# One transformer block on one core: the fourth block's statistics on ScalarE, two projections out of the front, four beside the first block's norm

## The chip, the cores and the metric

The kernel runs on one core of one Trainium2 chip. A core has four computing engines, TensorE (PE in the profile; its weight loads are listed apart as PEld), VectorE (DVE), ScalarE (ACT) and GpSimd (POOL), and SyncE (SP), which here issues nearly all DMA transfers. Each engine runs its own instructions in order and waits for the others by semaphores. The metric is the device time of one launch in microseconds, the median of some runs.

## The reference

Everything is float32. The inputs are x (1 x 2048 x 512), a condition c (1 x 512) and the weights.

```
mod = (silu(c) @ w_mod).reshape(1, 6, 1, 512)
sa, ca, ga, sb, cb, gb = mod[:, 0], ..., mod[:, 5]
h = layernorm(x) * (1 + ca) + sa
q, k, v = heads(h @ wqkv)                 # 32 heads of 16
p = softmax(q @ k.T * 16 ** -0.5)         # full, 2048 x 2048 for each head
x = x + ga * ((p @ v) @ wo)
h = layernorm(x) * (1 + cb) + sb
x = x + gb * (gelu(h @ w1 + b1) @ w2 + b2)   # 512 -> 1792 -> 512
```

## The kernel before, in words

The 2048 rows are cut into four blocks of 512 (b = 0 to 3). Numbers that need more than the array's reduced precision are split into a high and a low part, and a product is the sum of three products of parts; a 512 x 512-row piece of a projection is then 12 matmuls of 512 columns (`terms3`, line 276 issues them). Projections are named (w, k, b): w = 0 is Q, 1 is K, 2 is V; k is one of four groups of eight heads; b is the block of rows.

**The front** is an order written out by hand, `SCRIPT`, whose tokens are run in order, each on an engine that the token may name (.v VectorE, .a ScalarE, .g GpSimd). For the tokens that matter here: `Z` loads a block of x; `S` takes the statistics of 128 rows (line 237 and 238, VectorE); `F`, `P`, `B` make the factor and the offset of the norm; `N` normalizes 128 rows; `T` transposes; `H` modulates; `I` and `L` make the high and low part of h (line 484 is `L`); `G` is one projection on the whole array; `A`, `R`, `D`, `O` split and store its result (line 508 is `D`); `K` and `Q` load K and Q back in the layout of the attention; `X` issues a pair of matmuls of scores for the row maxima (line 390), and `x` one reduction of such a tile on VectorE (line 395). Results of projections go through DRAM: `store_qk` writes the parts (lines 298 and 299), `load_rows` reads them back (line 362). The front ends when 80 maxima matmuls (`LEAD`) and their reductions are issued. The projections of the front are those that the first two units need, and some more, 13 in all.

**The attention** is one loop of 512 half-steps. A unit u is a block of 512 query rows and a group of four heads (32 units, 16 half-steps each; unit u uses query block u // 8 and head group u % 8, so k = u % 8 // 2). In a half-step TensorE issues four score matmuls for the exponentials (line 647, ScalarE's exponentials are line 654), four score matmuls for the maxima of a later unit, 80 matmuls ahead, one group of eight matmuls with V (`pv_step`, line 681), and, between them, six matmuls of a job in the background on one half of the array's rows (`bg_mm`, line 276). A job with 12 terms thus takes four half-steps. A job starts only on an even half-step. A turn (four transposes) may be added to a half-step from the list `sides`.

The counter `clock["t"]` goes up by one with each exponential, so by four in a half-step. `later(n, f)` runs f after n of them, and `soon` does the same and counts it as owed. `step_start(s)` runs at the start of a step and issues the loads in `due` whose step has come and whose projections are stored: for unit u + 2 its Q and four quarters of K, for unit u + 1 two halves of V.

**The order of the jobs** is that of the generator `work()`: `block0()` gives the projections that the front left (35), then waits until the preparation of the weights, the divisions by the softmax sums and the stores are through, and opens the pools of the feed-forward; then come, for each block, `front(b)` (four output projections, the second norm, four turns) and `feed(b)` (the feed-forward). Where the generator gives None the half-step runs without a job. For block 0, `front` runs its four turns as pieces of their own, for blocks 1 and 2 they go into `sides` beside jobs. What is not done at the end of the loop runs after it, on the whole array, ahead of the last block's output projection.

Of the kernel before, what the change touches and what calls it, by code (L numbers as in the profile page):

```python
# [16 lines left out]
P = 128  # L17
# [30 lines left out]
lw10.g be F1 L01.v H02.a L03.g W11 L00.v I02.a S22 P1 L02.v G100 S21 B1 N10.a N11.g S20 G000 N13.a R100.v  # L48
N12.a A100.v S23 D100.g F2 S31 A000.a P2 O100 T12 D000.v B2 H12.a S30 O000 T10 N22.a I12.g N23.v T13 N20.a
H10.v hw01.g N21.a H13.v T11 I10.g lw01.v I13.a T22 L10.g L12.v H11.a W20 L13.v T20 hw11.a H22.a I11.g T21 K00  # L50
# [4 lines left out]
L33.g L31.v A010.a X0*3 x R010.a G103 x D010.g x*2 O010 x*2 R103.a X0*2 x X0 A103.a G203 x D103.g x*2 O103 x*2  # L55
A203.a X0*2 x X0 G201 x*4 K03 x A201.a X0*2 x X0 K13 U201 x*2 pa1 C201 x O201 va2 pb1 x*2 vb2 X0 c1.a X0*2 x
ml1 x G111 md1 x*4 A111.a X0*2 R111.a X0 G112 x D111.g x*2 O111 x*2 A112.a X0 x X0 R112.a pa2 x D112.g x pb2 x
O112 x c2.a X1*2 x X1 mb0 x om x mb1 me0.a x U203 me1.a x*2 C203 X1*2 x X1 O203 G202 x*3 lm x*2
Y202.a X1 x*2
# [11 lines left out]
def block_kernel(ctx: ExitStack, tc: tile.TileContext, x, wqkv, wo, w1, b1, w2, b2, c, w_mod, out):  # L71
# [73 lines left out]
    pccm, pcpool = pool("pc", side="right")  # L145
    hcm, hpool = pool("hT", side="right")

# [3 lines left out]
    hT = [[rows_tile(b, "hi", "hThi"), None] for b in range(NB)]  # L151
    xin = [None] * NB
    wcm, wpool = pool("wqk", side="right")
    wslots = [wpool.tile([P, 2, KC, P], FR, name=f"wqkv{i}") for i in range(4)]
# [21 lines left out]
    def load_x(b, q=sy):  # L176

        xin[b] = rows_tile(b, "lo", "xin", (P, 4, D), F32)
        for t in range(0, 4, 1 if b == 0 else 4):
            r0, n = b * TB + t * P, 1 if b == 0 else 4  # L180
            q.dma_start(xin[b][:, t : t + n], x[r0 : r0 + n * P, :].rearrange("(t p) d -> p t d", p=P))
# [111 lines left out]
    stored = set()  # L293

    def store_qk(w, k, b, parts):
        stored.add((w, k, b))
        planes = qk_d[w][k].rearrange("i d o t -> (d o) i t")[:, :, b * TB : (b + 1) * TB]
        sy.dma_start(planes[:, 1 - w : 3 - w], parts.bitcast(F32))
        sy.dma_start(planes[:, 2 * w], parts[:, 0].bitcast(F32))
# [30 lines left out]
    def turn_v(bk, apart=False):  # L330
# [12 lines left out]
        def store():  # L343
            stored.add((2, k, b))
            (ac if apart else sy).dma_start(v_d[2 * k : 2 * k + 2, :, 4 * b : 4 * b + 4, :].rearrange("g p k e -> p g k e"), vst)
# [106 lines left out]

    def power(b):
        gp.tensor_tensor(rs1[b], rs1[b], mhalf, op=ALU.pow)
# [26 lines left out]
    def low_x(b, f, e):  # L481
        if hT[b][1] is None:
            hT[b][1] = rows_tile(b, "lo", "hTlo")
        e.tensor_tensor(hT[b][1][:, f], keep.pop(("H", b, f)), hT[b][0][:, f].bitcast(F32), op=ALU.subtract)
# [73 lines left out]
    def high_later(w, k, b, e):  # L558
# [8 lines left out]
        "S": lambda b, t: ln_stat(mv1[b], t, xin[b][:, t]), "F": add_eps, "P": power, "B": offset, "N": norm1,  # L567
# [26 lines left out]
    vg, pt = {}, {}  # L594

    def load_v(u, h):
        assert all((2, u % NG // 2, b) in stored for b in (2 * h, 2 * h + 1))
        if h == 0:
            vg[u] = vgpool.tile([P, NKC, VG], F32, tag="vg", name="vg")
        sl = slice(8 * h, 8 * h + 8)  # L600
        sy.dma_start(vg[u][:, sl], v_d[u % NG][:, sl])

    load_v(0, 0)
# [70 lines left out]
    def pv_step():  # L674
        s = cur["pv"]
        cur["pv"] += 1
        u, kc = divmod(s, NKC)
        if kc == 0:
            cur["ps"] = take("pv")
# [137 lines left out]
    def front(b, x2):  # L817
# [9 lines left out]

        def norm(t):
            xn[t] = tmp("xn")
            (gp if b or t < 3 else ve).tensor_scalar(  # L830
                xn[t], x2[t], mv[:, t, 0:1], rs[t], op0=ALU.subtract, op1=ALU.mult)
            later(40, lambda: gp.tensor_tensor(x2[t], x2[t], b2_b, op=ALU.add))
            if b and len(xn) == 4:
                later(9, lambda: sides.extend([lambda fc=fc: trans(fc, "mx") for fc in range(KC)]))

        def stat(t):
            if b == 0 and t == 3:
                ln_stat(mv, t, x2[t])
                later(1, lambda: factor(t))
                return  # L840
# [10 lines left out]
            later(4, lambda: part(1))  # L851
            later(8, whole)

        def factor(t):
# [3 lines left out]
            later(3 if t < 3 else 2, lambda: norm(t))  # L858

        for t in range(4):  # L860

            def evac(ps, t=t):
# [3 lines left out]
                def add():  # L866
                    gp.tensor_tensor(x2[t], y, x2[t], op=ALU.add)
                    later(8 if b or t < 3 else 3, lambda: stat(t))
# [5 lines left out]
        t0 = clock["t"]  # L874

        def trans(fc, bk="bg"):
# [11 lines left out]
        if b:  # L888
            yield from until(lambda: len(turned) == KC and clock["t"] >= turned[KC - 1] + 8)
            return  # L890
        yield from until(lambda: len(xn) == 4 and clock["t"] >= t0 + 9)
        for fc in range(KC):
            yield lambda fc=fc: trans(fc)
        yield from wait(4)

    def feed(b, x2):
# [4 lines left out]
        def piece(i):  # L901
            return f.tile([P, 2, TB], FR, tag="g", name="g", bufs=8)
# [66 lines left out]
    def block0():  # L969

        plan = [(1, 1, [3]), (2, 1, [0, 1, 2, 3])]
        plan += [(w, k, range(1 if w == 0 else NB)) for k in (2, 3) for w in (0, 1, 2)]
        plan += [(0, k, range(1, NB)) for k in range(KC)]

        def fetch(n):
            if n < len(plan):
                w, k, _ = plan[n]
                load_w(w, k)
                soon(12, lambda: split_w(w, k, wslots[n % 4]))
# [3 lines left out]
        for n, (w, k, bs) in enumerate(plan):  # L983
            if not pcs and not any(0 in p[2] for p in plan[n:]):
                open_pc()
            yield from until(lambda: (w, k) in wt_of)
            fetch(n + 2)
            for b in bs:
                yield proj_v(k, b) if w == 2 else proj_qk(w, k, b)
            wt_of.pop((w, k))  # L990
        yield from until(lambda: not preps and not owed[0] and not vrows and not busy[0])
        open_ffn()
# [5 lines left out]
    def work():  # L998

        yield from block0()  # L1000
        fronts = [front(b, pools["x2"][b % 2]) for b in range(NB - 1)]
        for b in range(NB - 1):
            for j in fronts[b]:
                if j != "ln":
                    yield j
            for j in feed(b, pools["x2"][b % 2]):
# [39 lines left out]
    def half_step(hs):  # L1046
# [4 lines left out]
        h = hs % 2  # L1051
        if h or len(wt) < len(used) + KC:
            wload()
# [93 lines left out]
    due = [(1, [(2, 0, 2)], lambda: load_v(0, 1))]  # L1147

    def step_start(s):
        u, kc = divmod(s, NKC)  # L1150
        for d in [d for d in due if d[0] <= s and all(k in stored for k in d[1])]:
            due.remove(d)
            d[2]()
        if kc == 0 and u + 2 < NU:
            g = (u + 2) % NG // 2
            due.append((16 * u + 4, [(0, g, (u + 2) // NG)], lambda: load_q(u + 2)))
            for b, n in enumerate((5, 8, 14, 16)):
                t0 = b % 2 * TB
                due.append((16 * u + n, [(1, g, b)], lambda b=b, t0=t0: load_k(u + 2, b // 2, t0, t0 + TB)))
        if kc == 0 and u + 1 < NU:  # L1160
            for h in range(2):
                need = [(2, (u + 1) % NG // 2, b) for b in (2 * h, 2 * h + 1)]
                due.append((16 * u + 2 + h, need, lambda h=h: load_v(u + 1, h)))
# [116 lines left out]
    close(tcm, pools["cm"], pccm, kqcm)  # L1280
# [24 lines left out]
```

## Time and profile before

| | |
|---|---|
| median of 3 runs | 1687.93 us (1685.45 to 1688.35) |
| the profiled execution, its time | 1688.23 us |
| its span in the profile | 1686.4 us |
| mean granted TensorE clock | 0.996 |
| busy: TensorE, VectorE, ScalarE, GpSimd | 1666.6, 1402.0, 1242.7, 691.2 us |
| front, loop, tail (by the trace) | 0 to 100.35, to 1562.67, to 1686.40 us |

Busy time is the time in which an engine had an instruction in work. The chain of waits follows, from the last instruction back, what released each step; its shares tell where the span went. A line number belongs to the helper that issues the instruction, so the tile's names tell which step it is. Matmuls are pipelined, so TensorE's busy time doesn't say that it is at its peak.

### The profile page before, as it was taken

To read this page: it belongs to the slowest core of one execution; us is meant where nothing else is said; L and a number is where in the kernel's file an instruction comes from. 1 tells how busy PE (TensorE), PEld (TensorE's weight loads), DVE (VectorE), ACT (ScalarE), POOL (GpSimd) and SP (SyncE) were. 2 spreads that over 40 slices of the span, in tenths; PEclk is the share of its full clock that TensorE was granted. 3 is DMA by queue.
4 is the path that set the end of the run, shared out by engine and by line. 5 is a ranking of instruction groups with operands and counts; after the bars stand their busy time and mean duration, and the time that the engine had idled before them with its cause. 6 is when DMAs were issued, how large, how long until landed. Compare 5 with 4: busy or idle time off the path is not lost.

```text
span 1686.4 us, 32218 instructions
## 1 busy us (share of the span) xinstructions
PE 1666.6 (99%) x12103; PEld 915.8 (54%) x12103; DVE 1402.0 (83%) x2686; ACT 1242.7 (74%) x2386; POOL 691.2 (41%) x697
## 2 busy tenths in 40 slices
PE   7999999999999999999999999999999999999999
PEld 6655555555554455555545555555555555553777
DVE  7998888889889989888999888888999888890332
ACT  4367888878777788778877888778877788779131
POOL 7333534425121456415633456306633466226110
PEclk8999999999999999999999999999999999999999
DMA  8766766756457443425453464344363453243544
GB/s 291 220 195 186 236 194 200 227 182 206 146 159 215 121 106 102 106 67 150 123 162 88 114 165 121 84 133 134 105 181 86 116 144 101 75 119 97 209 153 157
DMA packets 137127, 251.88 MB, mean 149 GB/s; under 512 B 25854, under 2 KB 45324, under 8 KB 136972
## 3 DMA queue, kind: packets, MB, share of 16 engines
q1 hardware_dynamic: 135984, 248.53, 50.9%
q8 instruction: 96, 1.57, 0.4%
q10 hardware_dynamic: 988, 1.29, 0.3%
q14 instruction: 59, 0.48, 0.1%
HBM read 188.49 MB, written 61.28 MB: 148 GB/s over the span
## 4 chain that ended last, share of the span: by engine, by line
PE 95%; DMA 2%; DVE 1%; ACT 1%; issue 0%; POOL 0%; SPq 0%; DVEq 0%; POOLq 0%; ACTq 0%
PE bg L276 40%; PE pv L681 30%; PE e L647 16%; PE mx L390 5%; PE pr L276 2%; ACT p L654 1%; DVE mxp L395 1%; DMA wraw<-in_A_wqkv_dram 1%; PE o L276 1%; PE mx L335 0%; DMA wo<-wos 0%; DMA kh<-qk 0%; PE mx L879 0%; DMA xin<-in_A_x_dram 0%; POOL wqkv L208 0%
## 5 line engine op out<-in xcount | busy, mean ns | idle before, releaser
L395 DVE TENSOR_REDUCE mxp<-mx 128x1 f32<-128x512 f32 x2034 | 1286.4, 683 | 145.7 <-PE mx L390 131.4
L654 ACT ACTIVATE p<-e 128x512 f32<-128x512 f32 x2048 | 1072.8, 608 | 272.2 <-PE mx L390 251.4
L390 PE MATMUL mx<-kh,qst 48*128 48x512 f32 x2034 | 836.6, 423 | 0.7 <-DVE mxp L395 0.5
L647 PE MATMUL e<-qst,kh 50*128 50x512 f32 x2048 | 779.2, 424 | 3.2 <-ACT p L654 3.2
L647 PEld LDWEIGHTS e<-qst,kh 50*128 50x128 f32 x2048 | 341.8, 185 | 431.5 <-ACT p L654 310.2
L681 PE MATMUL pv<-p,vg 128*32 128x512 f32 x4096 | 547.2, 605 | 0.3 <-ACT osb L668 0.3
L390 PEld LDWEIGHTS mx<-kh,qst 48*128 48x128 f32 x2034 | 368.2, 185 | 14.2 <-DVE mxp L395 8.3
L276 PE MATMUL bg<-w,g 64*128 64x512 f32 (+1 forms) x1056 | 264.3, 389 | 0.8 <-issue 0.8
L276 PEld LDWEIGHTS bg<-w,g 64*128 64x128 f32 (+1 forms) x1056 | 196.0, 186 | 30.0 <-issue 1.2
L276 PE MATMUL bg<-pchi,w 64*128 64x512 f32 (+1 forms) x656 | 177.6, 391 | 0.0
L681 PEld LDWEIGHTS pv<-p,vg 128*32 128x32 f32 x4096 | 81.1, 108 | 173.0 <-issue 160.3
L276 PE MATMUL bg<-hThi,wqkv 64*128 64x512 f32 x560 | 153.1, 392 | 0.0
L276 PEld LDWEIGHTS bg<-pchi,w 64*128 64x128 f32 (+1 forms) x656 | 120.9, 185 | 23.9 <-DVE tick L1091 4.2
L276 PEld LDWEIGHTS bg<-hThi,wqkv 64*128 64x128 f32 x560 | 103.7, 185 | 12.7
L923 POOL TENSOR_SCALAR s<-s 128x512 f32<-128x512 f32 x40 | 59.9, 1497 | 90.3 <-ACT s L921 89.6
L942 POOL TENSOR_TENSOR x<-y,x 128x512 f32<-128x512 f32 x28 | 36.0, 1286 | 144.6 <-ACT y L941 128.7
L276 PE MATMUL bg<-pclo,w 64*128 64x512 f32 (+1 forms) x328 | 88.9, 389 | 0.0
L276 PE MATMUL bg<-hTlo,wqkv 64*128 64x512 f32 x280 | 76.5, 392 | 0.0
L276 PEld LDWEIGHTS bg<-pclo,w 64*128 64x128 f32 (+1 forms) x328 | 60.0, 184 | 13.5 <-DVE tick L1091 4.2
L916 POOL TENSOR_TENSOR s<-h 128x512 f32<-128x512 f32 x40 | 41.7, 1042 | 61.7 <-ACT h L915 61.7
L276 PE MATMUL bg<-wo,pchi 64*128 64x512 f32 x192 | 59.5, 389 | 0.4 <-DMA wo<-wos 0.4
L276 PEld LDWEIGHTS bg<-hTlo,wqkv 64*128 64x128 f32 x280 | 51.6, 184 | 7.5
(163 smaller groups left out, 1322.9 us busy)
## 6 DMA issues: line engine op xcount, KB each, us to landing
kh<-qk SPq DMA_DIRECT2D x256, 192.0 KB
w<-w1s SPq DMA_DIRECT2D x56, 512.0 KB
w<-w2s SPq DMA_DIRECT2D x54, 512.0 KB
vg<-v SPq DMA_DIRECT2D x64, 332.0 KB
qk<-parts SPq DMA_DIRECT2D x32, 512.0 KB
qst<-qk SPq DMA_DIRECT2D x64, 192.0 KB
qk<-parts SPq DMA_DIRECT2D x32, 256.0 KB
ou<-osb SPq DMA_DIRECT2D x32, 256.0 KB
```

The lines of the kernel that those rows point to most:

```text
L276: return te.matmul(ps, term[0][r], term[1][r], start=i == 0, stop=i == n - 1)
L390: te.matmul(ps, qst[u][r0 : r0 + KR, p, qc * P : (qc + 1) * P], kh(u, kr // 2)[r0 : r0 + KR, p, (kr % 2) * TB : (kr % 2 + 1) * TB], start= ...
L395: ins = ve.tensor_reduce(mxp[u][:, hc, kr : kr + 1], ps, axis=AX.X, op=ALU.max, negate=True)
L647: ins = te.matmul(ps, kh(u, kc // 8)[r0 : r0 + KX, p, (kc % 8) * P : (kc % 8 + 1) * P], qst[u][r0 : r0 + KX, p], start=True, stop=True)
L654: op = ac.activation(t, ps, AF.Exp, scale=SCALE)
L681: te.matmul(cur["ps"][32 * j : 32 * (j + 1)], vg[u][:, kc, j * VW : j * VW + 32], pt.pop(4 * s + j), start=kc == 0, stop=kc == NKC - 1)
L916: gp.tensor_tensor(s, h, h, op=ALU.mult)
L923: gp.tensor_scalar(s, s, 1.0, None, op0=ALU.add)
L942: later(4, lambda: gp.tensor_tensor(x2[t], y, x2[t], op=ALU.add))
```

## The change

In the front the sums and the sums of squares of the fourth block's rows are taken on ScalarE, by activations with a summed output (tokens `E`, `V`), and GpSimd and VectorE make mean and variance of them (`J`, `f`). The projections G111 and G112 (K of head group 1 for blocks 1 and 2) leave the front and become jobs of the loop. The reductions are spaced anew, and the first maxima matmuls come ahead of G110. The fourth block's h and the four weight slots lie in the eight tiles that the feed-forward uses later (`piece_tile`), so they may live past the opening of its pools. In the loop the order of the projections is written out, and the four Q projections of block 3 are set aside (`deferred`); they run wherever block 0's path would give None, and the pools are opened from the half-step itself (`try_open`). Block 0's norm of its last 128 rows takes its statistics in halves, normalizes on GpSimd, and its turns go into `sides`. Loads of K and Q now wait until six exponentials after the store's issue, those of V until four, and V is loaded in quarters for the units that need a fresh projection.

```diff
-N12.a A100.v S23 D100.g F2 S31 A000.a P2 O100 T12 D000.v B2 H12.a S30 O000 T10 N22.a I12.g N23.v T13 N20.a
+N12.a A100.v V30 V31 V32 S23 D100.g F2 A000.a P2 O100 T12 D000.v B2 H12.a O000 T10 N22.a I12.g N23.v T13 N20.a
...
-H20.a I22.g L11.v I20.a lw11.g T23 H21.a K10 S32 G101 I21.g Q0 H23.a L22.v I23.a Q1 L20.v L23.g G110 L21.v
-A101.a S33 hw20.a lw20.g F3 D101.v P3 R110.a X0*2 O101 A110.a x X0 B3 G200 x D110.g N32.a x N30.a x N31.g O110
+H20.a I22.g L11.v I20.a lw11.g T23 H21.a Q0 f3 G101 I21.g H23.a L22.v I23.a K10 L20.v L23.g X0*2 Q1 G110 x L21.v x
+A101.a hw20.a lw20.g x R101.a D101.g P3 R110.a X0 x O101 A110.a x X0*2 B3 G200 x D110.g N32.a x N30.a x N31.g O110
...
-ml1 x G111 md1 x*4 A111.a X0*2 R111.a X0 G112 x D111.g x*2 O111 x*2 A112.a X0 x X0 R112.a pa2 x D112.g x pb2 x
...
+    def row_sum(b, t):
+        o = kqpool.tile([P, TB], F32, tag="osb", name="junk", bufs=1)
+        ac.activation(o, xin[b][:, t], AF.Identity, accum_out=sums[:, 0, t : t + 1])
...
+    def row_var(b, t):
+        o = kqpool.tile([P, TB], F32, tag="osb", name="junk", bufs=1)
+        ac.activation(o, xin[b][:, t], AF.Square, bias=sums[:, 1, t : t + 1], accum_out=sums[:, 2, t : t + 1])
...
         def norm(t):
             xn[t] = tmp("xn")
-            (gp if b or t < 3 else ve).tensor_scalar(
-                xn[t], x2[t], mv[:, t, 0:1], rs[t], op0=ALU.subtract, op1=ALU.mult)
+            gp.tensor_scalar(xn[t], x2[t], mv[:, t, 0:1], rs[t], op0=ALU.subtract, op1=ALU.mult)
...
-            if b and len(xn) == 4:
-                later(9, lambda: sides.extend([lambda fc=fc: trans(fc, "mx") for fc in range(KC)]))
+            if len(xn) == 4:
+                later(9 if b else 6, lambda: sides.extend([lambda fc=fc: trans(fc, "mx") for fc in range(KC)]))
...
-            later(4, lambda: part(1))
-            later(8, whole)
+            later(2 if short(t) else 4, lambda: part(1))
+            later(4 if short(t) else 8, whole)
...
-        plan = [(1, 1, [3]), (2, 1, [0, 1, 2, 3])]
-        plan += [(w, k, range(1 if w == 0 else NB)) for k in (2, 3) for w in (0, 1, 2)]
-        plan += [(0, k, range(1, NB)) for k in range(KC)]
+        plan = [(1, 1), (2, 1), (0, 2), (1, 2), (2, 2), (0, 3), (1, 3), (2, 3)] + [(0, k) for k in range(KC)]
+        order = [(0, 1), (0, 2), (0, 3), (1, 0), (1, 1), (1, 2), (1, 3), (2, 0), (3, 0), (3, 1), (3, 2), (3, 3),
+                 (4, 0), (4, 1), (4, 2), (5, 0), (6, 0), (4, 3), (6, 1), (6, 2), (6, 3),
+                 (7, 0), (7, 1), (7, 2), (8, 1), (7, 3), (8, 2), (9, 1), (9, 2), (10, 1), (10, 2), (11, 1), (11, 2)]
...
+    def filled(js):
+        for j in js:
+            yield proj_late() if j is None and deferred else j
+
+    def try_open():
+        if over0[0] and "f" not in pools and not preps and not owed[0] and not vrows and not busy[0]:
+            open_ffn()
...
-        for d in [d for d in due if d[0] <= s and all(k in stored for k in d[1])]:
+        for d in [d for d in due if d[0] <= s and all(clock["t"] >= stored.get(k, 1 << 30) + d[2] for k in d[1])]:
             due.remove(d)
-            d[2]()
+            d[3]()
...
-                due.append((16 * u + n, [(1, g, b)], lambda b=b, t0=t0: load_k(u + 2, b // 2, t0, t0 + TB)))
+                due.append((16 * u + n, [(1, g, b)], 6, lambda b=b, t0=t0: load_k(u + 2, b // 2, t0, t0 + TB)))
```

In `order` each pair is a place in `plan` and a block of rows; counted from 0, the nth pair is the loop's nth job.

More of the change, by code (lines that the diff above doesn't have):

```diff
@@ L887, in front @@
         yield "ln"
[L888 to L894, printed above, removed]
+        yield from until(lambda: len(turned) == KC and clock["t"] >= turned[KC - 1] + (8 if b else 5))
     def feed(b, x2):
@@ L991, in block0 @@
-        yield from until(lambda: not preps and not owed[0] and not vrows and not busy[0])
-        open_ffn()
+            yield from until(lambda: plan[n] in wt_of)
+            fetch()
+            w, k = plan[n]
+            yield proj_v(k, b) if w == 2 else proj_qk(w, k, b)
+            left.pop(0)
+            if n not in left and n < len(plan) - KC:
+                wt_of.pop((w, k))
+        deferred.extend((k, gslots[(len(plan) - KC + k) % 4]) for k in range(KC))
+        over0[0] = True
@@ L1051, in half_step @@
         h = hs % 2
+        try_open()
         if h or len(wt) < len(used) + KC:
```

138 lines of the change are left out of this document (87 added, 51 removed).

## The prediction

> **What bounds the kernel now.** I read the page first, then the share of each engine by stretch, then the chain of waits, then single instructions on VectorE's, ScalarE's and SyncE's timelines.
>
> ```profile
> span 1686.4 us, 32218 instructions
> PE 1666.6 (99%) x12103; PEld 915.8 (54%) x12103; DVE 1402.0 (83%) x2686; ACT 1242.7 (74%) x2386; POOL 691.2 (41%) x697
> PE 95%; DMA 2%; DVE 1%; ACT 1%; issue 0%; POOL 0%; SPq 0%; DVEq 0%; POOLq 0%; ACTq 0%
> ```
>
> TensorE is busy 99% of the span and carries 95% of the chain, so the kernel falls into stages that all end with TensorE, and a moved piece is worth what its old place gives back less what its new place takes.
>
> ```profile
> 0.00:47.42 47.42, 38.50 (x211) 30.06 (x213) 38.51 (x68) 20.44 (x31) 36.59 (x45) 0.89 0.87 277
> 47.42:100.35 52.93, 51.94 (x259) 32.17 (x255) 50.07 (x86) 18.70 (x35) 15.36 (x17) 1.00 0.71 221
> 100.35:1562.67 1462.32, 1457.37 (x11116) 757.67 (x11116) 1273.48 (x2469) 1176.56 (x2282) 627.71 (x626) 1.00 0.50 140
> ```
>
> The columns are stretch, length, then busy time (and instructions) of PE, PEld, DVE, ACT, POOL. In the second row, the half of the front that holds the row maxima, TensorE works 51.94 of 52.93 us, but VectorE works 50.07. Two limits lie 1.9 us apart there: taking work from TensorE alone soon uncovers VectorE. In the attention (third row) VectorE has room: 1273 of 1462 us.
>
> **The change part by part.**
>
> *Two projections leave the front (G111, G112).* A projection there is 12 matmuls, alone on the array:
>
> ```profile
> 47.84 3.00 PE pr L276 x12
> 40.53 0.68 DVE L237 BATCH_NORM_STATS2 bst<-xin 128x6 f32<-128x512 f32 x1
> 41.34 3.92 DVE L484 TENSOR_TENSOR hTlo<-h,hThi 128x512 fp32r<-128x512 f32 x3
> 45.18 0.68 DVE L237 BATCH_NORM_STATS2 bst<-xin 128x6 f32<-128x512 f32 x1
> 46.12 0.58 DVE L451 TENSOR_SCALAR rs<-mv 128x4 f32<-128x4 f32 x1
> 46.62 0.68 DVE L508 TENSOR_TENSOR parts<-pr,parts 128x512 fp32r<-128x512 f32 x1
> 47.42 3.68 DVE L395 TENSOR_REDUCE mxp<-mx 128x1 f32<-128x512 f32 x6
> ```
>
> On TensorE 2 x 3.00 = 6.0 us go. The 80 row-maximum matmuls and their 80 reductions stay in the front, respaced. VectorE loses four statistics (0.68 each and an aggregate), one rest (0.68) and one subtraction that goes to GpSimd; one subtraction that stood before the first reduction (a third of the 3.92 us, 1.31) now comes after it, and the one that leaves the second stretch is taken at 0.91 by me (an estimate between the 0.68 and the 1.31). So from the first reduction to the loop VectorE has 50.07 - 0.91 + 1.31 = 50.5 us of work. The first maximum matmuls now stand behind one projection (G101) and not two, so the first reduction comes about 2.8 us earlier (3.00, less an estimated 0.2 for Q's rows, whose load SyncE now puts out just ahead of their use). If VectorE idles in between as much as before (52.93 - 50.07 = 2.9), the front ends 2.8 - 0.4 = 2.4 us earlier; if it idles not at all, 5.3. That is all of the 6.0 that can be had.
>
> *ScalarE takes the fourth block's statistics.* Four sums, four squares. The nearest rows are its normalizations, also with pointers for scale and offset:
>
> ```profile
> 31.23 0.60 ACT L192 ACTIVATE parts<-pr 128x512 fp32r<-128x512 f32 x1 [1.80 <-PE pr L276]
> 32.72 2.23 ACT L464 ACTIVATE xin<-xin,nb,rs 128x512 f32<-128x512 f32 x3 [0.23 <-POOL nb L459]
> ```
>
> That is 0.74 us each; the sum that is written out as well is in no row, so I bound one at 0.60 to 1.00 and take 0.85. The four sums go into an earlier gap. Three squares stand ahead of the evacuation at 31.23, in a gap of 1.80: 3 x 0.85 - 1.80 = 0.75 us late (0 to 1.2). Behind it wait the rest on VectorE, the bank, and the transposition that needs the bank; the fourth square then stands ahead of the third block's modulations. VectorE's missing statistics give part of this back. I charge 0.9 us to all that follows (0 to 1.5). The two small GpSimd operations and the split load of x on SyncE lie under the sums. The front is worth 2.4 - 0.9 = -1.5 us (from -5.3 to +0.2).
>
> The Trainium skill (ScalarE: Activation LUTs, What ACT_TABLE_LOAD costs) prices an ACTIVATE with one pointer at 280 ns + 0.833 ns an element, less 93 ns back to back: 0.61 us here, an estimate that leaves out the written sum. By it the three squares about fit the 1.80 gap and the front would be worth some 2.3 us; the rows at 0.74 speak against so little.
>
> *The stretch around the first block's norm.* In the loop a projection takes four half-steps (24 half-row matmuls, six each). Before: 35 projections fill half-steps 0 to 139, six half-steps idle (the last store, then the loads of wo), 146 to 161 hold four output projections, and eight idle ones hold the norm, with four turns.
>
> ```profile
> 484.88:507.65 22.77, 22.77 (x182) 11.94 (x178) 20.54 (x40) 17.51 (x35) 7.00 (x8) 1.00 0.43 134
> 507.65:523.47 15.82, 14.37 (x102) 5.00 (x98) 15.09 (x27) 13.13 (x26) 2.12 (x4) 1.00 0.57 171
> 523.47:569.98 46.51, 46.11 (x358) 24.06 (x354) 43.43 (x89) 35.37 (x69) 9.56 (x9) 1.00 0.59 163
> 569.98:594.88 24.90, 23.40 (x150) 9.04 (x146) 21.84 (x39) 19.55 (x37) 13.93 (x14) 0.93 0.63 155
> 509.39:512.00 2.61, 2.40 (x20) 0.83 (x24) 2.53 (x5) 2.07 (x5) 0.46 (x3) 1.00 0.08 13
> 583.54:586.44 2.90, 2.90 (x25) 1.25 (x22) 2.33 (x4) 2.37 (x5) 1.53 (x3) 1.00 0.45 138
> 528.22:531.72 3.50, 3.10 (x27) 1.33 (x30) 2.90 (x6) 2.44 (x6) 0.00 (x0) 1.00 1.04 406
> 584.50 0.59 PE bg L879 x4
> 1562.67 16.57 PE bg L276 x72
> 1580.06 3.01 PE bg L276 x12
> ```
>
> A filled half-step costs 22.77 / 8 = 2.85 us, an idle one 2.61, an idle one with a turn 2.90: filling an idle slot costs 0.24 us. That is why moving work here is cheap. After: 33 projections (0 to 131); three of the four deferred ones until the store, the softmax divisions, four ticks and the loads of wo are through (132 to 143); outputs 144 to 159; the last deferred one 160 to 163. By the new delays the first turn comes 20 exponentials, five half-steps, after the last output; turns at 164 to 167, two idle, and the feed-forward starts at 170, as before. So the jobs behind it stay, and the number that overrun the loop (84 / 12 = 7 of 12 matmuls, the last two rows). Sum over 132 to 169: 12 x 2.85 + (46.51 - 0.65 for the load of wo that ended late, the 3.50 us half-step) + 4 x 2.85 + 4 x 3.05 + 2 x 2.61 = 108.9, against 22.77 + 15.82 + 46.51 + 24.90 = 110.0: -1.1 us. A turn goes at 3.05, between 2.90 and 2.61 + 0.59 of transposes; -1.8 to +1.5 if new norm waits show. The halved statistics and GpSimd's normalization of the fourth row go under deferred work; without that cover they cost what the 24.90 row has over 8 x 2.61, up to 4 us.
>
> *What the two late projections do to SyncE.* All K and V of the loop come up to eight half-steps later, and loads now also wait six exponentials after the store. The maxima run 80 ahead, 4 a half-step; unit 6 needs K of its second 512 rows at 6 x 64 + 16 = 400 = 80 + 4 x 80, half-step 80. That K projection now is job 18, half-steps 72 to 75. Before, job 18 was the K of the fourth rows, so its rows show when such a load can go out:
>
> ```profile
> 100.35:333.82 233.47, 84.17 (x632) 12.45 (x632) 1.00 0.68 206
> 321.45 0.60 ACT L310 ACTIVATE pf<-bg 128x512 f32<-128x512 f32 x1
> 326.84 0.57 SPq L422 DMA_DIRECT2D qst<-m  x2
> 327.92 0.43 SPq L298 DMA_DIRECT2D qk<-parts  x1
> 328.40 0.45 SPq L299 DMA_DIRECT2D qk<-parts  x1
> 332.65 2.13 SPq L362 DMA_DIRECT2D kh<-qk  x2
> SPq L362 <- DMA qk<-parts: 1.4, 2, 0.9
> 53.09 1.74 SPq L362 DMA_DIRECT2D kh<-qk  x4
> 57.66 0.29 PEld L390 LDWEIGHTS mx<-kh,qst 48*128 48x128 f32 x3 [0.17 <-DMA kh<-qk]
> ```
>
> 632 / 8 = 79 PV groups have run by 333.82: there half-step 80 starts. The store goes out at 327.92, behind the maxima's rows; the load waited for it until 332.65. Before, its data had until half-step 88. Now they are wanted at once: with the 57.66 - 53.09 = 4.57 us from issue to use seen in the front they land at 337.2, 3.3 us late. TensorE stands, with everything behind it. Bounds: 0, if the load goes out earlier, to three times 3.3 (the third and fourth rows' K, half-steps 84 and 88, have the same distance, but the first stand gives them its 3.3 us and no maxima's rows are in front of them: I charge them 0.2). V of units 4 and 6, loaded in quarters, has over two half-steps: nothing; the two more issues a unit (0.45 us each, as at 328.40) fit SyncE's gaps.
>
> The Trainium skill (DMA: Bandwidth & Descriptors, Anatomy of one DMA) gives 2.0 us + bytes / 436e3 per DMA; two of 192 KB, one issue apart, would land about 2.9 us after the first issue, an estimate for another issuing path. By it the stand is 1.8 us and the sum 1687.6; the trace's 4.57 decides.
>
> *Sum.* -1.5 - 1.1 + 3.3 + 0.2 = +0.9 us on the profiled execution's 1688.23, that is 1689.1; it lies 0.3 above the median 1687.93, so 1688.8. No change that a measurement can tell: about 0.2%, 3.4 us, is what it resolves here.
>
> **The rivals.** *The K load is in time* (SyncE runs ahead of TensorE, and the store finds no maxima's rows in front): then -1.5 - 1.1 = -2.6; with half of VectorE's 2.9 us of idling gone too, -4.1, 1683.8, faster. For it: in the waits of 320 to 345 us, the quoted row, SyncE stood 0.9 us at the longest for such a store. Against: 332.65 is a measured time for this very slot. Chance 0.26.
>
> *The K loads are late again and again*, slower: the second and third stand full as well, 3 x 3.3 - 2.6 = +7.3, 1695.2; it decides from the second on (+4.0, 1691.9). For it: evacuation at 321.45 to issue at 332.65 is 11.2 us, and with 4.57 more 15.8; the four half-steps between are 11.4. Against: in the other two nothing holds the store back but GpSimd. Chance 0.26. The Trainium skill (same page and section) says that a DMA's completion is told only when its last byte is confirmed in the target memory, long above all with HBM; the 4.73 us from store to dependent load agree.
>
> *ScalarE's statistics eat the front*: one at 1.0 us with VectorE idle as before, front +0.2; then 1690.5, still no change. Chance 0.08.
>
> **Chances.** The forecast (one stand of about 3 us, front and middle some 2.6) 0.40, with 0.08 for the last rival: 0.48 within 0.2%. Faster 0.26, slower 0.26. Range 1683.0 to 1693.5: the low end takes the K load in time with part of the front's bound, the high end two full stands and a little more.
>
> **What the profile would show.** Right: VectorE without a gap before the loop, the loop's first exponentials 1 to 2 us earlier; a wait of TensorE's maxima on the K load near half-step 80; half-steps 132 to 143 all full; no wait on wo; the feed-forward at half-step 170. Wrong: no such wait; a front shorter by over 3 us; an overrun of the loop by six jobs or eight instead of seven.

## The result, and the profile after

The change made the kernel slower. The median went from 1688.14 us (four runs, 1685.45 to 1688.77) to 1710.76 us (four runs, 1703.86 to 1712.29); the ratio is 1.0129, with a 95% interval of 1.0100 to 1.0159. The prediction was 1688.8 us, with a range from 1683.0 to 1693.5. The profiled execution took 1712.29 us, at a mean granted clock of 0.989 (0.996 before).

From the page of the changed kernel: the span, the busy time by engine, the chain by engine, and the group of the maxima's matmuls (at the end of that row: the idle time of TensorE just ahead of them, and what ended most of it).

```profile
span 1710.5 us, 32286 instructions
PE 1676.3 (98%) x12127; PEld 922.1 (54%) x12127; DVE 1396.8 (82%) x2682; ACT 1248.5 (73%) x2401; POOL 697.4 (41%) x704
PE 91%; DMA 4%; ACT 2%; DVE 1%; POOL 1%; issue 1%; SPq 0%; DVEq 0%; POOLq 0%; ACTq 0%
L414 PE MATMUL mx<-kh,qst 48*128 48x512 f32 x2038 | 842.7, 424 | 17.1 <-DMA kh<-qk 14.3
```

TensorE is busy 10 us longer than before, although the two projections only changed their place (in the loop each is 24 matmuls on half of the array's rows), and the chain now runs through transfers for 4% of the span (2% before). The maxima (line 414, line 390 before) stood 14.3 us for K. By stretch (columns as in the prediction; until the first reduction, then until the loop, then the loop):

```profile
0.00:44.25 44.25, 35.26 (x199) 27.53 (x199) 32.78 (x58) 24.96 (x46) 35.52 (x45) 0.92 0.88 291
44.25:112.15 67.90, 55.03 (x250) 33.50 (x247) 50.27 (x86) 18.61 (x34) 20.09 (x20) 0.90 0.52 157
112.15:1587.79 1475.64, 1467.45 (x11164) 765.18 (x11164) 1273.73 (x2475) 1177.90 (x2283) 630.26 (x629) 0.99 0.49 140
```

The span grew by 24.1 us. The first reduction comes 3.2 us earlier, but the stretch from there to the loop takes 67.90 us and not 52.93, with the same 50 us of VectorE's work in it: VectorE idles 17.6 us. The loop takes 13.3 us more, the rest, the tail, 1.0 less.

The front on TensorE, instructions in order of time (start, length; in brackets the idle time ahead and what ended it):

```profile
57.36 1.05 PE L414 MATMUL mx<-kh,qst 48*128 48x512 f32 x6 [2.11 <-DMA kh<-qk]
...
69.52 0.60 PE L414 MATMUL mx<-kh,qst 48*128 48x512 f32 x2 [2.02 <-DMA kh<-qk]
70.05 3.18 PE L300 MATMUL pr<-h,wqkv 128*128 128x512 f32 x8
...
86.79 1.31 PE L414 MATMUL mx<-kh,qst 48*128 48x512 f32 x4 [5.09 <-DMA kh<-qk]
...
91.93 3.36 PE L300 MATMUL pr<-hThi,wqkv 128*128 128x512 f32 x8
...
104.33 2.11 PE L300 MATMUL pr<-hThi,wqkv 128*128 128x512 f32 x8
...
112.15 0.79 PE L414 MATMUL mx<-kh,qst 48*128 48x512 f32 x1 [2.27 <-DVE mxp L419]
...
119.75 1.93 PE L724 MATMUL pv<-p,vg 128*32 128x512 f32 x8
```

Three of the waits are for K of unit 0's second, third and fourth 512 rows; the fourth is for a reduction on VectorE. And eight matmuls of a projection, 2.11 us at 104.33, take 3.18 and 3.36 us behind two of the waits. The granted clock (the third number from the end of a row) shows why; behind the fourth wait the loop's first steps are slow too:

```profile
70.00:80.00 10.00, 10.00 (x45) 6.81 (x48) 5.99 (x10) 1.68 (x3) 1.29 (x1) 0.83 0.40 150
70.78:74.20 3.42, 3.42 (x10) 2.66 (x9) 0.54 (x1) 0.00 (x0) 0.00 (x0) 0.50 0.57 214
80.00:90.00 10.00, 4.91 (x27) 2.91 (x20) 4.61 (x9) 0.60 (x1) 0.00 (x0) 0.72 0.65 178
111.74:121.98 10.24, 9.83 (x41) 5.58 (x43) 6.62 (x12) 4.73 (x9) 0.19 (x1) 0.50 0.22 70
```

The clock is at one half from 70.78 to 74.20, from 84.44 to 94.68 and from 111.74 to 121.98 us, that is for 3.4 us or three times that.

The chain of waits through the third stand, step by step:

```profile
75.92 1.30 POOL parts L549
...
77.24 0.36 SPq L322
...
77.65 5.04 DMA qk<-parts
...
83.11 3.54 DMA kh<-qk
...
86.79 1.31 PE mx L414 x4
```

K goes from a projection to its maxima through memory: split, store (5.04 us until it is confirmed), load (3.54 us), 12.1 us from the projection's end (74.67) to the use. In the kernel before the way is as long: K of the second rows is used some 13.7 us after the end of its projection in both kernels (at 57.66 before, a row of the prediction, at 57.36 now). Before, other work filled it.

The loop: half-steps 80, 84 and 88, in which the maxima on unit 6's second, third and fourth rows begin, and 81, behind the first of them (a filled half-step is 2.85 us, with a turn 3.50):

```profile
349.05:355.48 6.43, 3.89 (x25) 2.03 (x23) 3.10 (x6) 3.25 (x7) 4.75 (x5) 0.89 0.46 134
355.48:359.28 3.80, 3.80 (x23) 1.60 (x23) 2.06 (x5) 2.08 (x5) 0.22 (x1) 0.73 0.09 36
364.97:369.35 4.38, 3.29 (x24) 1.73 (x22) 2.50 (x6) 2.90 (x7) 1.88 (x2) 1.00 1.04 263
377.99:384.83 6.84, 5.38 (x27) 3.15 (x27) 3.94 (x7) 3.62 (x7) 2.22 (x3) 0.75 0.84 248
```

Over 2.85 us (3.50 for the last, which holds a turn) that is 3.6 + 0.9 + 1.5 + 3.3 = 9.3 us; with 0.5 at half-step 60 and 0.2 at 92 the loop lost 10.0 us on K. TensorE's waits for K are 2.54, 1.09 and 1.46 us of this; the clock is at one half again from 354.09 to 357.50 and from 381.40 to 384.81 us. Four more it lost at its start, at the low clock: 7.6 us from 112.15 to the first PV group (4.5 before) and 1.0 in the half-step after it.

### The profile page after: what moved, and what is told of

Its sections match the earlier page's. It is cut to its first block, busy times and chain, and to the rows that moved or that the text cites. A ratio compares the mean times of both kernels' runs of the same rounds, so it can differ in the third digit from the quotient of the medians.

```text
span 1710.5 us, 32286 instructions
## 1 busy us (share of the span) xinstructions
PE 1676.3 (98%) x12127; PEld 922.1 (54%) x12127; DVE 1396.8 (82%) x2682; ACT 1248.5 (73%) x2401; POOL 697.4 (41%) x704
## 4 chain that ended last, share of the span: by engine, by line
PE 91%; DMA 4%; ACT 2%; DVE 1%; POOL 1%; issue 1%; SPq 0%; DVEq 0%; POOLq 0%; ACTq 0%
PE bg L300 39%; PE pv L724 29%; PE e L689 15%; PE mx L414 5%; DMA qk<-parts 1%; DMA kh<-qk 1%; ACT p L696 1%; DVE mxp L419 1%; PE pr L300 1%; DMA wraw<-in_A_wqkv_dram 1%; PE o L300 1%; PE mx L359 1%; PE mx L919 0%; DMA wf<-in_B_w_dram 0%; ACT xin L505 0%
## 5 line engine op out<-in xcount | busy, mean ns | idle before, releaser
L414 PE MATMUL mx<-kh,qst 48*128 48x512 f32 x2038 | 842.7, 424 | 17.1 <-DMA kh<-qk 14.3
L300 PEld LDWEIGHTS bg<-pchi,w 64*128 64x128 f32 (+1 forms) x656 | 120.9, 185 | 24.1 <-DVE tick L1157 4.2
L300 PE MATMUL bg<-hThi,wqkv 64*128 64x512 f32 x432 | 120.5, 400 | 0.0
L300 PEld LDWEIGHTS bg<-hThi,wqkv 64*128 64x128 f32 x432 | 82.1, 191 | 10.2
L435 POOL CAST m<-mt 128x32 fp32r<-128x32 f32 x32 | 6.7, 209 | 145.5 <-DVE mt L433 145.5
L300 PE MATMUL bg<-hTlo,wqkv 64*128 64x512 f32 x216 | 58.0, 388 | 0.0
```

What stands on the lines that cost most here:

```text
L300: return te.matmul(ps, term[0][r], term[1][r], start=i == 0, stop=i == n - 1)
L414: te.matmul(ps, qst[u][r0 : r0 + KR, p, qc * P : (qc + 1) * P], kh(u, kr // 2)[r0 : r0 + KR, p, (kr % 2) * TB : (kr % 2 + 1) * TB], start= ...
L435: gp.tensor_copy(m2[:, 0], mt)
```

## The experiments

All ratios are to the kernel before, run on the same chip in the same series, with 95% intervals.

**1. The front whole again, two jobs less in the loop.** The front's order of before stands in the changed kernel; the late Q projections, the pools' opening, the delays and V in quarters stay.

```diff
-        order = [(0, 1), (0, 2), (0, 3), (1, 0), (1, 1), (1, 2), (1, 3), (2, 0), (3, 0), (3, 1), (3, 2), (3, 3),
+        order = [(0, 3), (1, 0), (1, 1), (1, 2), (1, 3), (2, 0), (3, 0), (3, 1), (3, 2), (3, 3),
```

> Edit: the changed kernel with the front's order of before (13 projections, all statistics on VectorE) and without the two extra jobs in the loop; the four late projections of the first block and the new loads stay. Theory (all of the loss comes from the two projections that left the front): no maximum waits over 0.6 us for K in the front or in half-steps 60 to 92; the front as before, the stretch of half-steps 132 to 169 as in the changed kernel, 0.7 us shorter than before; about 1687.4 us. Rival (the late four, the quartered V loads or the longer delays cost time by themselves): stands remain in the loop, 1692 or more.

Measured: 1688.64 us, ratio 1.0008 (0.9999 to 1.0018): no difference. From its page: all maxima together stood 1.1 us, most of it for reductions, none to speak of for K.

```profile
L414 PE MATMUL mx<-kh,qst 48*128 48x512 f32 x2030 | 834.9, 422 | 1.1 <-DVE mxp L419 1.0
```

So the loss hangs on the two projections that left the front, with the order that the front was given for it. The late four, the delays and V in quarters cost nothing that can be measured, and bring nothing either.

**2. The front whole, all 33 jobs in the loop.** Only the front's order is that of before.

> Edit: the changed kernel with the front's order of before, all 13 projections in it, while the loop still holds all 33 of its jobs, so that two projections are computed twice (the loop's copies overwrite equal rows). It has the loop of the changed kernel behind the front of before. Theory (the loop's stands come from the two jobs more, whatever the front does): first PV group at 104 to 105 us, waits of the maxima on K at half-steps 60, 80, 84 and 88 as in the changed kernel, 8 to 10 us together; about 1696 us. Rival (the front's lateness pushes SyncE and GpSimd back, and the loop's stands come from that): stands under 3 us together, 1690 or less.

Measured: 1695.72 us, ratio 1.0051 (1.0036 to 1.0065). First PV group at 103.86 us, and the stands are there, with the low clock behind the first:

```profile
331.86:338.00 6.14, 3.29 (x25) 1.72 (x23) 2.49 (x6) 2.89 (x7) 4.27 (x5) 1.00 0.49 125
338.00:342.42 4.42, 4.42 (x23) 2.03 (x23) 2.90 (x6) 2.77 (x7) 0.68 (x1) 0.61 0.26 103
```

From half-step 60 to 92 the loop fell back 7.4 us, so most of the loop's loss does not come from the front. With experiment 1 this splits the result: 0.43% (some 7 us) for the two jobs more in the loop, 0.78% (1.0129 less 1.0051, some 13 us) for the front; the interval of the changed kernel's ratio alone leaves 5 us to either side of the second.

**3. Another order of the maxima in the front.** Three pairs of unit 1 (K there already) take the place of the first pairs on unit 0's second rows.

```diff
-N33.a x*2 A200.a X0*2 x X0 G102 K01 x*2 K11 x*3 A102.a X0*2 x X1 T30 D102.v x O102 T32 H30.a x I30.g T33 H32.a
+N33.a x*2 A200.a X0*2 x X0 G102 K01 x*2 K11 x*3 A102.a X1*2 x X1 T30 D102.v x O102 T32 H30.a x I30.g T33 H32.a
...
-X0 pa2 x X0 pb2 x*3 c2.a mb0 om me0.a X1*2 mb1 x X1 me1.a x*2 G202 lm x*3 X1*2 Y202.a x*2 X1*2 x*6
+X0 pa2 x X0 pb2 x*3 c2.a mb0 me0.a X0*2 mb1 x X1 me1.a x*3 om G202 lm x*2 X1*2 Y202.a x*2 X1*2 x*6
```

> Edit: the changed kernel with another order of the same 40 pairs of maxima in the front: three of unit 1, whose K is there, stand where the first maxima on unit 0's second rows stood; unit 0's last two come later for it. Theory (TensorE runs into loads of its own fresh K, and runs at half clock after each stand): the stands of 2.1, 2.0 and 5.1 us go or shrink to under 1.5 us together, no record at a clock of 0.5 between 65 and 105 us, first PV group 9 to 13 us earlier than 119.75; some 1699 us, since the loop's stands stay. Rival (VectorE is the bound and the stands only show it): the waits turn into waits on reductions, first PV group less than 4 us earlier, 1708 or more.

Measured: 1699.33 us, ratio 1.0071 (1.0056 to 1.0086), first PV group at 109.44. Two of the three stands are gone, the third is 2.21 us:

```profile
81.43 1.31 PE L414 MATMUL mx<-kh,qst 48*128 48x512 f32 x4 [2.21 <-DMA kh<-qk]
```

With the same work on every engine, an order in which TensorE asks for fresh K later gives back some 10 us: 1.0129 less 1.0071 is 0.58%, and the first PV group comes 10.3 us earlier (8.2 earlier than in the profile of experiment 6, whose front is the changed kernel's). (The clock behind the third stand still fell, to 0.66 in the mean of 80 to 90 us, which was expected not to happen.) VectorE was not the bound.

**4 and 5. The waits filled.** Small matmuls of no use ahead of the three waiting maxima (`WARM`: 12, 12, 30, then 9, 8, 21).

```diff
+        for n in range(WARM.get((u, i), 0) * a):
+            te.matmul(ps[:, :P], ident, ident, start=True, stop=True)
```

> Edit: the changed kernel with 12, 12 and 30 small matmuls (128x128 on the identity, about 0.15 us each) ahead of the three maxima of the front that wait for K, into the bank that these overwrite. They do no work; the data come no earlier. Theory (the clock falls because TensorE idles): no record at 0.5 between 65 and 105 us, the projections at 70.05 and 91.93 take 3.0 us instead of 4.6 and 4.2, and the first PV group starts 3 to 6 us earlier; 1705 to 1708 us. Rival (the clock falls for another reason): the records stay, and the time is that of the changed kernel or more.

> Edit: the changed kernel with 9, 8 and 21 small matmuls of no use ahead of the three maxima of the front that wait for K (12, 12 and 30 ran over the arrival of the last K by 3 us: each leaves two records of 0.115 us). Theory (TensorE's idling makes the clock fall; with the stands filled to 0.3 us each it does not): granted clock 1.00 from 50 to 105 us, the maxima on the last K at 86 to 87 us as in the changed kernel, the first PV group 3 to 4 us earlier than 119.75; some 1707 us. Rival (the fall of the clock costs nothing, since VectorE's reductions bound that stretch): first PV group at 119 us or later, 1710 or more.

Measured: 1708.49 us (1.0126, 1.0111 to 1.0141) and 1706.74 us (1.0111, 1.0098 to 1.0125). In the first the filling ended at 89.68 us, some 3 us behind the start of those maxima in the changed kernel (86.79), so its gain was given away and the expected time missed. The second, by stretch:

```profile
70.00:80.00 10.00, 9.80 (x54) 6.93 (x57) 7.20 (x12) 1.69 (x3) 2.82 (x3) 1.00 0.39 139
80.00:90.00 10.00, 10.00 (x80) 7.29 (x73) 6.27 (x13) 1.26 (x3) 0.00 (x0) 1.00 0.80 248
```

The clock stays at 1.00 where the changed kernel had 0.83 and 0.72, the maxima on the last K start at 86.93 us, no earlier than before, and the first PV group starts at 116.34 us, 3.4 earlier. How much of this is the clock is less sure than it looks: in the profile of experiment 6 the same front brought the first PV group at 117.61. That kernel's four times, taken in the same series, lie 3.4 us higher in the median (1710.15) and don't overlap with these, but its loop lost 1.7 us more. So of the front's 15 us some 1.3 to 3.4 were the low clock behind the K waits, and that clock follows TensorE's idling. The Trainium skill (TensorE: Matmul & The Clock Gate, Part 1: The HAM clock gate, and Why this matters for your kernels) says that the clock halves after an idle window of about 3.4 us and advises against gaps over some 3 us; the trace agrees with the half rate and with 3.4 us as its step, but here stands of 1.46 to 2.54 us were enough in several places (not in all: the first, 2.11 us, left the clock at 1.00).

**6. No delay ahead of the K loads.**

```diff
-                due.append((16 * u + n, [(1, g, b)], 6, lambda b=b, t0=t0: load_k(u + 2, b // 2, t0, t0 + TB)))
+                due.append((16 * u + n, [(1, g, b)], 0, lambda b=b, t0=t0: load_k(u + 2, b // 2, t0, t0 + TB)))
```

> Edit: the changed kernel in which the loop's K loads no longer wait six exponentials after the issue of their store (they still wait for its landing). Theory (job, evacuation, split, store and landing are too long a chain for four or five half-steps, and the delay lies beside the store's landing of 3 to 5 us): the stands at half-steps 60 to 92 change by less than 2 us in sum; 1709 to 1711 us. Rival (the added delay makes the stands): each shrinks by the 4 us of six exponentials, to under 3 us in sum; 1703 or less.

Measured: 1710.15 us, ratio 1.0133 (1.0120 to 1.0146). Half-steps 60 to 92 lost 11.7 us, no less than with the delay. The chain itself is too long:

```profile
337.77 0.67 ACT pf L334
...
339.18 1.29 POOL parts L336
...
344.31 0.42 SPq L322
...
344.79 4.09 DMA qk<-parts
...
349.32 3.62 DMA kh<-qk
...
353.08 0.47 PE mx L414
```

These are lines of the changed kernel's chain. From evacuation to use 15.3 us pass, of which four half-steps (11.4 us) are there; 3.8 us of it SyncE's queue holds the finished store back, behind the rows of the maxima (`m`, `qst`) and a weight.

**7. One projection back in the front.**

```diff
-c1.a X0*2 x X0 ml1 x*2 md1 U201 x*2 C201 x O201
+G112 c1.a A112.a R112.a X0*2 x D112.g X0 ml1 x*2 md1 O112 U201 x*2 C201 x O201
...
-        order = [(0, 1), (0, 2), (0, 3), (1, 0), (1, 1), (1, 2), (1, 3), (2, 0), (3, 0), (3, 1), (3, 2), (3, 3),
+        order = [(0, 1), (0, 3), (1, 0), (1, 1), (1, 2), (1, 3), (2, 0), (3, 0), (3, 1), (3, 2), (3, 3),
```

> Edit: the changed kernel with one of the two projections (second head group, third rows) back in the front, ahead of the maxima that wait 5.1 us, and out of the loop's list. Theory (with one more job in the loop unit 6's K is in time, with two it is not): the stands at half-steps 80, 84 and 88 go (under 0.5 us each), the loop gives back 8 to 10 us; the front's own stands stay, though the new projection fills 3 of the 5.1 us; about 1700 us. Rival (unit 6's K is late because of SyncE's order or of the six exponentials of delay, not for the one job more): stands of over 1 us remain at half-steps 80 and 84, 1705 or more.

Measured: 1705.45 us, ratio 1.0103 (1.0086 to 1.0120). The loop's stands on K are gone, as the theory had it (the front keeps two, of 2.03 and 1.97 us); but the time is the rival's, for a new stand came (half-steps 80 and 144; then, in order of time, GpSimd's division and the first scores behind it):

```profile
346.31:349.16 2.85, 2.85 (x25) 1.51 (x24) 2.48 (x5) 2.55 (x6) 2.77 (x3) 1.00 0.58 164
531.63:540.61 8.98, 4.45 (x26) 2.92 (x24) 3.28 (x6) 3.31 (x7) 2.21 (x4) 0.67 0.72 211
```

```profile
526.31 1.28 POOL L790 TENSOR_TENSOR ob<-ob,rb 128x512 f32<-128x512 f32 x1 [14.64 <-DMA rb<-rden]
...
537.22 0.76 PE L689 MATMUL e<-qst,kh 50*128 50x512 f32 x1 [4.53 <-DMA qst<-m]
```

GpSimd stood 14.64 us for the sums of a softmax division (2.04 us in the changed kernel), the cast of unit 9's maxima stood behind it, and the first scores of unit 9 waited for them.

**8. to 11. A version without these stands.** Experiment 8 joins the order of 3 with the projection of 7, and issues the divisions later; 9 also moves the fourth rows' chain forward in the front; 10 holds the loads of the feed-forward's weights back until the divisions are issued; 11 respaces the front's end.

```diff
-            later(9 if over[0] else 7, div)
+            later(9 if over[0] else 12, div)
```

> Edit: the changed kernel with the other order of maxima, one projection back in the front ahead of the maxima on the last K (and out of the loop), and GpSimd's softmax divisions issued five exponentials later, so that GpSimd does not stand in front of the cast of unit 9's maxima. Theory (both causes are mended: no loads of fresh K in the front, unit 6's K in time, and the stand at half-step 144 was GpSimd's queue): no wait over 1 us for K anywhere, none at half-step 144; first PV group at 107 to 109 us, and from there on within 1.5 us of before; 1689 to 1692 us. Rival (the loop holds a further cost of the late projections): a stand over 2 us elsewhere, 1694 or more.

Measured: 1703.68 us, ratio 1.0102 (1.0085 to 1.0119): a miss. K waits are under 0.4 us, but the stand at half-step 144 stayed (7.94 us), so a later issue of the division was no cure, and the front lost time to a load of `w_mod` that the earlier order now met (1.93 us, with a clock of 0.58 from 90 to 100 us): its first PV group came at 115.36 us, not at 107 to 109.

The front of experiment 9, shortened to the tokens that move:

```diff
-A101.a hw20.a lw20.g x R101.a D101.g P3 R110.a X0 x O101 A110.a x X0*2 B3 G200 x D110.g N32.a x N30.a x N31.g O110
+A101.a hw20.a lw20.g x R101.a D101.g R110.a X0 x O101 A110.a x X0*2 N32.a N30.a G200 x D110.g x x N31.g O110
...
-L33.g L31.g A010.a X0*3 x R010.a G103 x D010.g x*2 O010 x*2 R103.a X0*2 x X0 A103.a G203 x D103.g x*2 O103 x*2
+I33.g H31.a x X0*2 x U200 x L32.g C200 x O200 K12 X0*2 x I31.g L33.g L31.g G103 x K02 x*3 R103.a A103.a X0*3 x G010 x D103.g x*2
```

> Edit: as the kernel with both causes mended, and the fourth rows' chain earlier: their power and offset on GpSimd ahead of the first maxima, their transposes ahead of the third rows' K projection, and their K projection ahead of the second head group's Q, so that the last K is stored and loaded earlier. Theory (what bounds the start of the loop now is the round trip of the last K): maxima on the last K 2 to 4 us earlier than in the kernel with both causes mended, first PV group at 104.5 to 107 us; 1686 to 1689 us, about the time of before. Rival (VectorE's 50 us of work bound it): first PV group as in that kernel, within 1 us.

Measured: 1700.59 us, ratio 1.0092 (1.0077 to 1.0107). No wait for K is left in the front, and the first PV group starts at 109.31 us, later than expected; the stand at half-step 144 was 10.16 us. SyncE's queue of this kernel, ahead of that stand:

```profile
502.52 2.98 SPq L857 DMA_DIRECT2D x<-in_A_x_dram  x4
...
506.93 0.33 SPq L775 DMA_DIRECT2D rden<-dn  x1
...
513.80 0.61 SPq L781 DMA_DIRECT2D rb<-rden  x1
...
518.43 1.29 POOL L789 TENSOR_TENSOR ob<-ob,rb 128x512 f32<-128x512 f32 x1 [15.76 <-DMA rb<-rden]
```

With one job less the feed-forward's loads go out earlier, ahead of the two transfers that the division waits for (16 and 256 KB).

```diff
-        if over0[0] and "f" not in pools and not preps and not owed[0] and not vrows and not busy[0]:
+        if over0[0] and "f" not in pools and not preps and not owed[0] and not vrows and not busy[0] and done[0] == KC - 1:
```

> Edit: the kernel with the last rows first, GpSimd's divisions at their old distance, and the loads of wo, x and w1 for the first block's output held back until all four softmax divisions of that block are issued. Theory (with one job less these loads, some 3 MB, go out ahead of the divisions' small loads on SyncE; GpSimd waits 15 us for the last of those, and the cast of unit 9's maxima stands behind it): the stand at half-step 144 goes, the rest stays; 1691 to 1693 us. Rival (the stand has to do with the maxima of unit 9 themselves): it stays, 1699 or more.

Measured: 1692.72 us, ratio 1.0035 (1.0022 to 1.0048), as expected. Half-step 144 is an ordinary one, 2.85 us. What is left lies in the front: the first PV group comes at 110.84 us, 5.95 later than before, and from there on the profile is 2.0 us shorter than before.

```diff
-X0 pa2 x X0 pb2 x*3 c2.a mb0 me0.a X0*2 mb1 x X1 me1.a x*3 om G202 lm x*2 X1*2 Y202.a x*2 X1*2 x*6
+X0 pa2 x X0 pb2 x*3 c2.a X0*2 mb0 me0.a x mb1 X1 me1.a x*3 om X1 G202 lm x*4 X1*2 Y202.a x*2 X1 x*4
```

> Edit: as the one before, and the end of the front respaced: one pair of unit 1's maxima ahead of the last V projection instead of behind it, two of unit 0's pairs ahead of the broadcast that waits 0.72 us for ScalarE. Theory (in the last 10 us VectorE idles 2 to 3 us and then has seven reductions in a row, 4.3 us, which TensorE awaits): no wait over 0.8 us for a reduction before the loop, granted clock 1.00 from 100 to 110 us, first PV group at 104.5 to 107 us; 1686.5 to 1689 us, which would make a front of twelve projections as long as that of thirteen and no version faster than before. Rival (the round trip of unit 0's maxima through memory sets the start): first PV group at 108 us or later, 1691 or more.

Measured: 1693.11 us, ratio 1.0031 (1.0020 to 1.0042), the rival's time. TensorE's last wait for a reduction is shorter (0.40 us, 1.24 in experiment 10), but the first scores now wait longer for unit 0's maxima themselves (1.65 us instead of 0.79), and the clock is low again (0.70 in the mean from 95.21 us to the first PV group at 109.46):

```profile
100.77 0.66 PE L688 MATMUL e<-qst,kh 50*128 50x512 f32 x1 [1.65 <-DMA qst<-m]
```

No version with a projection less in the front came down to the kernel before; what holds the front of twelve back was not taken apart further.

**12. The statistics alone**, on the kernel of experiment 1: the tokens `S3`, `F3` are replaced by `E`, `J`, `V`, `f` at the change's places.

> Edit: on the kernel with the whole front and without the two loop jobs (1688.6 us), the fourth block's statistics go to ScalarE as in the change; nothing else. Theory (four sums and four squares at 0.75 and 0.83 us lie in ScalarE's gaps, and TensorE bounds this front): first PV group within 0.7 us of that kernel's 104.03; 1688 to 1689 us. Rival of the prediction (the squares ahead of the first evacuations push the front back by 0.75 us and more): first PV group at 104.8 or later, 1689.5 or more.

Measured: 1688.84 us, ratio 1.0011 (1.0002 to 1.0020), beside 1.0008 without: nothing that can be told apart. Its profiled execution (1694.08 us) was its slowest, with the first PV group late, at 105.93 us, the rival's time; one such execution decides nothing.

## Why the prediction was wrong

**The front's term (-1.5 us) failed; it was +13 to +15.** Its parts were right: the first reduction came 3.2 us earlier (2.8 predicted, less the 0.9 for ScalarE), VectorE's work from there to the loop is 50.27 us (50.5). The step that failed is "If VectorE idles in between as much as before", that is 2.9 us: it idled 17.6 us. I bounded the front by the sums of busy time and never asked when the data of the respaced maxima arrive. The sign was in a row that I quoted: K of the second rows was used at 57.66 after a wait of 0.17 us, so that round trip was just covered already. What covered the trips was the order of the front, not the two projections. From the kernel before, in order of time, the last projection ahead of the fourth rows' maxima (G201), these maxima, G111 and G112:

```profile
73.03 2.13 PE L276 MATMUL pr<-hThi,wqkv 128*128 128x512 f32 x8
...
79.37 1.43 PE L390 MATMUL mx<-kh,qst 48*128 48x512 f32 x6
...
81.64 2.12 PE L276 MATMUL pr<-hThi,wqkv 128*128 128x512 f32 x8
...
85.52 2.13 PE L276 MATMUL pr<-hThi,wqkv 128*128 128x512 f32 x8
```

G111 and G112 stood behind the first use of the last K, so they covered none of the three trips. In the new order the maxima come before the work that stood ahead of them: three turns (2.0 us, at 55.55 and 56.53 before, at 58.34 and 59.21 now) for the second rows, G103 (3.0, at 65.02 before, at 70.05 now) for the third, G201 (3.0, at 73.03 before, at 91.93 now) for the fourth. Together these are 8.0 us, against 9.2 us of waits. Experiment 3, which changes only the order, gives back 8 to 10 us.

**The low clock was no term at all.** The prediction has no price for what follows a wait; it is 1.3 to 3.4 us behind the front's K waits (experiment 5), some 4 at the loop's start, where TensorE had waited 2.27 us for a reduction, and in the loop's half-steps 80 to 88 part of the 4.2 us by which the loss of 9.3 exceeds the waits of 5.1.

**The K loads of unit 6 (+3.3 and +0.2) were mis-sized: 10.0 us in the profile, some 7 by experiments 1 and 2.** Mechanism, place and the first stand were right (half-step 80 is 3.6 us too long). Wrong was that "the first stand gives them its 3.3 us": the third and fourth rows stood as well, 1.5 and 3.3 us. That is the rival "late again and again", which put three full stands at 3 x 3.3 = 9.9 us (7.3 is its sum with the -2.6 of the front and the middle). A stand delays the next projection along with its use, since TensorE runs both, so little is gained on it (argued, not tested by itself), and one store ahead of the last stand took 7.63 us to land:

```profile
369.42 7.63 DMA qk<-parts
...
377.47 3.33 DMA kh<-qk
```

The delay of six exponentials plays no part (experiment 6); one job less in the loop frees the way (experiment 7). The Trainium skill (DMA: Bandwidth & Descriptors, Anatomy of one DMA) gives 2.6 us for a store of 256 KB, an estimate by its formula, which is for another issuing path. Here a projection's result goes out in a store of 512 KB and one of 256 KB behind it (lines 322 and 323), and the chains show 3.37, 3.87, 4.09, 5.04 and 7.63 us from the issue of the second; the measurement decides.

**The stretch around the norm (-1.1) was right in its direction, at -0.5:** half-steps 132 to 169 took 109.49 us (509.77 to 619.26) instead of 110.0 (in the profiles of experiments 1 and 10 the same stretch is 0.8 and 1.5 us shorter than before). Half-steps 140 to 144 are all filled, and at half-step 148 there is no wait for wo:

```profile
532.49:546.72 14.23, 14.23 (x112) 7.59 (x110) 12.93 (x27) 11.30 (x23) 4.22 (x6) 1.00 0.65 196
555.36:558.21 2.85, 2.85 (x25) 1.50 (x23) 2.49 (x5) 2.56 (x6) 1.28 (x1) 1.00 1.07 340
```

**ScalarE's statistics were right in price and overcharged in effect.** A square comes every 0.83 to 0.85 us (0.85 taken):

```profile
30.82 0.72 ACT L489 ACTIVATE junk<-x,sums 128x512 f32<-128x512 f32 x1
31.45 0.19 ACT L489 ACTIVATION_READ_ACCUMULATOR junk<-x,sums 128x1 f32 x1
31.54 0.58 ACT L216 ACTIVATE parts<-pr 128x512 fp32r<-128x512 f32 x1
```

The evacuation behind them starts at 31.54 instead of 31.23, 0.3 us later and not 0.75. The 0.9 us charged to all that follows cannot be seen in the changed kernel, whose first reduction is 3.2 us earlier and not 1.9; experiment 12, with intervals of some 1.5 us to either side, can't tell it from nothing.

## What to carry to other kernels

Before work is taken out of a stretch or put in another order, list each round trip of data through memory in it, with its slack and with the work that covers it, not only the engines' busy sums: work that looks like load on a busy engine may be the cover of a transfer, and a wait of 0.2 us on a load says that the cover is used up. Price a new wait of TensorE with the time that it then runs at a lower clock. And a schedule written to the half-step has such limits in several queues at once: one job less moved a burst of loads ahead of two transfers that a division waited for and stopped the core for 6 us, far from the edit.

## What the runs showed of the hardware

Waits of TensorE of 1.46 to 2.54 us, and not only the long one of 5.09, were followed by stretches at a granted clock of one half (70.78 to 74.20, 84.44 to 94.68, 111.74 to 121.98, 354.09 to 357.50 and 381.40 to 384.81 us in the changed kernel: each 3.4 us or three times that), while waits of 2.11 and 1.09 us were not; useless matmuls in the front's K waits kept it at 1.00 from 50 to 105 us. An activation with a summed output is two instructions, the second a read of the accumulator of 0.19 us. Where the changed kernel's trace shows when a projection's store had landed, it was 3.4 to 5.6 us after the issue of its second part, but 7.63 and 7.26 us in two places (issued at 369.42 and 422.07); behind the first of them stands the longest half-step of the loop, 6.84 us.
